# Four tokens to a partition, half-array scores with one Exp over two banks, first batch transposed by the PE, and every engine ordered by a time model

## Chip, cores and metric

The kernel runs on one core of a Trainium2 chip. The metric is the device time of one execution in microseconds (us); medians of several executions are quoted. The engines are PE (TensorE: matmuls, and PEld for its weight loads), ACT (ScalarE), DVE (VectorE), POOL (GpSimd) and SP (SyncE, which here only issues DMAs). Each takes its instructions in a fixed order.

## The reference, cut

```python
# q, k, v: (8 batches, 12 heads, 448 tokens, 64) f32;  w_in: (768, 2048), w_out: (2048, 768) f32
q_n, k_n = rmsnorm(q, g_q), rmsnorm(k, g_k)          # over the 64 of a head
attn = softmax(q_n @ k_n.T / 8)                      # 448 x 448 for each head
x = (attn @ v) as (8*448, 768)
h = x @ w_in
out = (h * clip(h + 3, 0, 6) / 6) @ w_out            # (3584, 768) f32
```

Heads are worked on in 48 pairs, six to a batch. Attention of a batch must be complete before the first h matmul of that batch, because h contracts over all twelve heads.

## The kernel before

448 tokens are cut as 3 x 128 + 64. The 64 left over take a path of their own (loads, norms, a transpose and zero-padded copies for two batches at a time). A pair has seven score matmuls of 128 rows; since a head has 64, the keys are multiplied by a mask, so that the other head's 64 rows are zero.

```python
def pad_pair(P):                       # keys of a pair, twice, each with the other head zeroed
    ...
    nc.vector.tensor_copy(out=kq[:, 2 * SM:], in_=st["rT", b // 2][:, 1, j, e:e + 64])
    for a in range(2):
        nc.vector.tensor_scalar_mul(kp[:, a, :], kq[:, 0:SM], gmask[:, a:a + 1])

def score(P, u):                       # u = 0..6
    ...
    ps = ps_S.tile([128, S], FP32, name="s_ps")
    nc.tensor.matmul(out=ps[:], lhsT=lhsT, rhs=st["qT", P], start=True, stop=True)
    nc.scalar.activation(out=st["e", P][:, u, :], in_=ps[:], func=EXP, bias=zero_c[:], scale=1.0)

def trans_pair(P):                     # every transpose is a DMA transpose
    nc.sync.dma_start_transpose(out=kq[:, 0:2 * SM]..., in_=qks[:]...)

ps_S = pool("ps_S", 3, space=PSUM); ps_X = pool("ps_X", 1, space=PSUM)
ps_R = pool("ps_R", 1, space=PSUM); ps_M = pool("ps_M", 3, space=PSUM)     # M: h and y

# order: SP and POOL by hand; attention and the h and y groups merged by their shares of columns
with tc.manual_schedule(engines={mybir.EngineType.SP, mybir.EngineType.Pool}):
    for b in range(B):
        att = [...]                                                 # attention of batch b
        mlp = mlp_items(h_items(b - 1), y_items(b - 2) ..., 2)      # h of b-1, y of b-2
        for _, fn in merge(att, mlp):
            fn()
    ...
# the weights are loaded between the pairs: w_in at pairs 0 to 6, w_out at pairs 8 to 11
```

Of the kernel before, what the change touches and what calls it, by code (L numbers as in the profile page):

```python
# [10 lines left out]
A_MULT = mybir.AluOpType.mult  # L11
A_ADD = mybir.AluOpType.add
A_MIN = mybir.AluOpType.min
# [4 lines left out]
PSUM = bass.MemoryType.PSUM  # L18


@with_exitstack
def kernel(
# [11 lines left out]
    nc = tc.nc  # L34
# [3 lines left out]
    NPAIR = H // 2  # L38
    NT = 3
    SM = NT * 128  # L40
    SR = S - SM
    NKT = DM // 128
    NFT = DFF // 128
    NU = 2 * NT + 1
    E1 = D + 1
    E2 = 2 * E1
    HALF = DM // 2
    assert SR == 64 and D == 64 and NKT == NPAIR and B % 2 == 0

    pool = lambda name, bufs, **kw: ctx.enter_context(tc.tile_pool(name=name, bufs=bufs, **kw))  # L50
    const = pool("const", 1)


    gq_t = const.tile([128, 1], FP32, name="gq_t")
    gk_t = const.tile([128, 1], FP32, name="gk_t")
    for a in range(2):
        nc.gpsimd.dma_start(out=gq_t[a * 64:(a + 1) * 64, :], in_=g_q.rearrange("(p o) -> p o", o=1))
        nc.gpsimd.dma_start(out=gk_t[a * 64:(a + 1) * 64, :], in_=g_k.rearrange("(p o) -> p o", o=1))
    mask = const.tile([128, 2], FP32, name="mask")
    nc.gpsimd.memset(mask[:], 0.0)  # L60
    nc.gpsimd.memset(mask[0:64, 0:1], 1.0)
    nc.gpsimd.memset(mask[64:128, 1:2], 1.0)
    gprime = const.tile([128, 1], FP32, name="gprime")
    gmask = const.tile([128, 2], FP32, name="gmask")

    def make_gmask():
        nc.vector.tensor_mul(gprime[:], gq_t[:], gk_t[:])
        nc.vector.tensor_scalar(gmask[:], mask[:], gprime[:], 8.0, A_MULT, A_MULT)

    half_c = const.tile([128, 1], FP32, name="half_c")  # L70
    nc.gpsimd.memset(half_c[:], 0.5)
    zero_c = const.tile([128, 1], FP32, name="zero_c")
    nc.gpsimd.memset(zero_c[:], 0.0)

    eps_c = const.tile([128, 1], FP32, name="eps_c")
    nc.gpsimd.memset(eps_c[:], D * 1e-6)
    nc.scalar.preload_act_table_set("natural_log_exp_and_others")

# [3 lines left out]
    NVA = 4  # L82
    va_ring = []
    for i in range(NVA):
        t = const.tile([128, 2, NT, E1], BF16, name=f"va{i}")
        nc.gpsimd.memset(t[:, :, :, D:E1], 1.0)
        va_ring.append(t)
    NVB = 3
    vbd_ring = []
    for i in range(NVB):  # L90
        t = const.tile([128, NPAIR, E2], BF16, name=f"vbd{i}")
        for a in range(2):
            c = a * E1 + D
            nc.vector.tensor_copy(
                out=t[:, :, c:c + 1],
                in_=mask[:, a:a + 1].unsqueeze(1).to_broadcast([128, NPAIR, 1]),
            )
        vbd_ring.append(t)


    qk_pool = pool("qk_pool", 5)
    v_pool = pool("v_pool", 4)
    sq_pool = pool("sq_pool", 2)
    st_pool = pool("st_pool", 8)
    qks_pool = pool("qks_pool", 4)
    rst_pool = pool("rst_pool", 1)
    vr_pool = pool("vr_pool", 2)
    rT_pool = pool("rT_pool", 2)
    kq_pool = pool("kq_pool", 4)
    kp_pool = pool("kp_pool", 3)  # L110
    kbd_pool = pool("kbd_pool", 3)
    e_pool = pool("e_pool", 3)
    rd_pool = pool("rd_pool", 3)
    xn_pool = pool("xn_pool", 3)
    xr_pool = pool("xr_pool", 2)
    xT_pool = pool("xT_pool", 1)
    g_pool = pool("g_pool", 1)
    t_pool = pool("t_pool", 2)
    y_pool = pool("y_pool", 4)
    ps_S = pool("ps_S", 3, space=PSUM)  # L120
    ps_X = pool("ps_X", 1, space=PSUM)
    ps_R = pool("ps_R", 1, space=PSUM)
    ps_M = pool("ps_M", 3, space=PSUM)

    st = {}


    def rstd_of(ssq, n):
        rs = st_pool.tile([128, n], FP32, name="rs", tag="rs")
        nc.scalar.activation(out=rs[:], in_=ssq, func=LN, bias=eps_c[:])  # L130
        nc.scalar.activation(out=rs[:], in_=rs[:], func=EXP, bias=zero_c[:], scale=-0.5)  # L131
        return rs

    def square(out, x, early):
        if early:
            nc.scalar.square(out=out, in_=x)
        else:
            nc.gpsimd.tensor_tensor(out=out, in0=x, in1=x, op=A_MULT)  # L138

    def load_qk(P):  # L140
        b, j = divmod(P, NPAIR)
        hs = slice(2 * j, 2 * j + 2)
        qk = qk_pool.tile([128, 2, 2, NT * D], FP32, name="qk")
        for i, src in enumerate((k, q)):
            nc.sync.dma_start(  # L145
                out=qk[:, i], in_=src[b, hs, 0:SM, :].rearrange("h (p t) d -> p h (t d)", t=NT))
        st["qk", P] = qk

    def load_v(P):
        b, j = divmod(P, NPAIR)  # L150
        vf = v_pool.tile([128, 2, NT * D], FP32, name="vf")
        nc.sync.dma_start(
            out=vf[:],
            in_=v[b, 2 * j:2 * j + 2, 0:SM, :].rearrange("h (p t) d -> p h (t d)", t=NT))
        st["vf", P] = vf

    def load_pair(P):
        load_qk(P)
        load_v(P)

    def norm_pair(P):
        qk = st["qk", P]
        sq = sq_pool.tile([128, 4 * NT * D], FP32, name="sq", tag="sq")
        square(sq[:], qk[:].rearrange("p a h x -> p (a h x)"), P < 4)
        ssq = st_pool.tile([128, 4 * NT], FP32, name="ssq", tag="ssq")
        nc.vector.tensor_reduce(  # L166
            out=ssq[:], in_=sq[:].rearrange("p (n d) -> p n d", d=D), axis=AX_X, op=A_ADD)
        st["ssq", P] = ssq

    def rstd_pair(P):  # L170
        st["rs", P] = rstd_of(st.pop(("ssq", P))[:], 4 * NT)

    def prep_qk(P):
        qk, rs = st.pop(("qk", P)), st.pop(("rs", P))
        rs4 = rs[:].rearrange("p (a h t) -> p a h t", a=2, h=2)
        qks = qks_pool.tile([128, 2, NT, 2, D], BF16, name="qks")
        for i in range(2):
            nc.gpsimd.tensor_tensor(  # L178
                out=qks[:, i].rearrange("p t h d -> p h t d"),
                in0=qk[:, i].rearrange("p h (t d) -> p h t d", d=D),  # L180
                in1=rs4[:, i].unsqueeze(3).to_broadcast([128, 2, NT, D]),
                op=A_MULT)
        st["qks", P] = qks

    def prep_v(P):
        vf = st.pop(("vf", P))
        va = va_ring[P % NVA]
        nc.gpsimd.tensor_copy(  # L188
            out=va[:, :, :, 0:D], in_=vf[:].rearrange("p h (t d) -> p h t d", d=D))
        st["va", P] = va  # L190

    def prep_pair(P):
        prep_qk(P)
        prep_v(P)


    def load_rest(b, i):
        if i == 0:
            st["qkr", b] = rst_pool.tile([128, 2, H, D], FP32, name="qkr")
        for e in range(2):  # L200
            (nc.scalar if b == 0 and i == 1 else nc.sync).dma_start(
                out=st["qkr", b][e * 64:(e + 1) * 64, i],
                in_=(k, q)[i][b + e, :, SM:S, :].rearrange("h p d -> p h d"))

    def load_vrest(b):
        vr = vr_pool.tile([128, NPAIR, D], FP32, name="vr")
        vv = v[b, :, SM:S, :].rearrange("(j a) p d -> a p j d", a=2)
        for a in range(2):
            (nc.scalar if b == 0 else nc.sync).dma_start(out=vr[a * 64:(a + 1) * 64], in_=vv[a])
        st["vr", b] = vr  # L210

    def prep_vrest(b, a):
        vr = st["vr", b]
        vbd = vbd_ring[b % NVB]
        nc.gpsimd.tensor_scalar(
            vbd[:, :, a * E1:a * E1 + D], vr[:], mask[:, a:a + 1], None, A_MULT)
        st["vbd", b] = vbd

    def norm_rest(b, i):
        sq = sq_pool.tile([128, 4 * NT * D], FP32, name="sqr", tag="sq")  # L220
        square(sq[:], st["qkr", b][:, i].rearrange("p h d -> p (h d)"), b == 0)
        ssq = st_pool.tile([128, H], FP32, name="ssqr", tag="ssq")
        nc.vector.tensor_reduce(
            out=ssq[:], in_=sq[:].rearrange("p (n d) -> p n d", d=D), axis=AX_X, op=A_ADD)
        st["ssqr", b, i] = ssq

    def rstd_rest(b, i):
        st["rsr", b, i] = rstd_of(st.pop(("ssqr", b, i))[:], H)

    def prep_rest(b, i):  # L230
        if i == 0:
            st["qkrs", b] = rst_pool.tile([128, 2, H, D], BF16, name="qkrs")
# [11 lines left out]
    def pad_rest(b):  # L244
        e = b % 2
        kbd = kbd_pool.tile([128, NPAIR, 128], BF16, name="kbd")
        for a in range(2):
            nc.vector.tensor_scalar_mul(  # L248
                kbd[:, :, a * 64:(a + 1) * 64], st["rT", b // 2][:, 0, :, e * 64:(e + 1) * 64],
                gmask[:, a:a + 1])  # L250
        st["kbd", b] = kbd


    def trans_pair(P):
        qks = st.pop(("qks", P))
        kq = kq_pool.tile([128, SM + S], BF16, name="kq")
# [354 lines left out]
```

## Time and profile before

| | before |
|---|---|
| time, median of 3 | 531.95 us |
| span of the profiled run | 532.4 us |
| PE busy | 438.5 us (82%) |
| ACT / DVE / POOL busy | 299 / 286 / 214 us |
| columns in all matmuls | 938,500 = 391 us at 2.4 columns/ns |

Busy time of PE overlaps from matmul to matmul, so columns and the distance from start to start say more than its busy share. (2.4 is a round figure: in these traces matmuls of 384 columns start 162 ns apart and those of 512 columns 216 ns, which is 2.37 columns/ns.)

The page's 40 slices (13.3 us each) show in tenths how busy PE was, the clock it was granted, and the mean busy share of the DMA engines. The first nine have full DMA engines.

```profile
...
PE   0365565769988985999889997889978999999996
...
PEclk9987867888999999799998998999989999999999
DMA  9899999996658375435769365446664132120012
```

The windows view gives for each stretch its length, then busy us (and instructions) of PE, PEld, DVE, ACT and POOL, then the PE clock, the DMA share (1 is all 16 engines) and GB/s. The first h matmul of batch 1 starts at 132.8 us, and the last value matmul at 470.0 us.

```profile
...
20.00:60.00 40.00, 24.25 (x193) 13.65 (x192) 30.33 (x42) 25.76 (x54) 28.71 (x33) 0.83 1.08 213
60.00:132.00 72.00, 49.66 (x386) 29.10 (x387) 47.92 (x76) 44.34 (x94) 42.64 (x46) 0.81 0.99 175
132.00:470.00 338.00, 306.23 (x2443) 179.52 (x2442) 178.72 (x377) 209.05 (x403) 132.12 (x142) 0.97 0.53 116
470.00:533.00 63.00, 57.84 (x330) 31.59 (x326) 20.93 (x35) 11.58 (x17) 0.00 (x0) 1.00 0.16 50
...
```

The groups view of the page (line, engine, operation, shapes, count, then busy us, mean ns, idle us before) shows the Exps and the scores of the main path:

```profile
...
L286 ACT ACTIVATE eT<-s_ps,zero_c 128x448 bf16<-128x448 f32 x336 | 202.7, 634 | 79.7 <-PE s_ps L285 78.8
...
L285 PE MATMUL s_ps<-kq,kp 128*128 128x448 bf16 x288 | 109.1, 387 | 30.6 <-DVE kp L269 30.0
...
```

In the timeline of PE (start us, us, instruction) a score matmul of 448 columns (L285) is followed by the next work 0.18 to 0.19 us later, about what 448 columns take at 2.4 columns/ns (187 ns). The four y matmuls ahead of it hold PE for 0.65 us (164.17 to 164.82), four times 162 ns:

```profile
...
163.99 0.35 PE L285 MATMUL s_ps<-kq,kbd 128*128 128x448 bf16 x1
164.17 0.81 PE L388 MATMUL y_ps<-w_out_sb,gT 128*128 128x384 bf16 x4
164.82 0.35 PE L285 MATMUL s_ps<-kq,kp 128*128 128x448 bf16 x1
165.01 0.81 PE L388 MATMUL y_ps<-w_out_sb,gT 128*128 128x384 bf16 x4
...
```

The chain of waits (the work that ended last, followed back) has 45% on PE, 18% on DMA and 12% in which an engine waited for nothing that the profile shows:

```profile
...
PE 45%; DMA 18%; issue 12%; DVE 11%; POOL 8%; SPq 3%; ACT 1%; POOLq 0%
...
```

The groups by shape give the price of ACT work: 128 columns more cost 106 ns.

```profile
...
L374 ACT ACTIVATE t_sb<-h_ps,half_c 128x512 f32<-128x512 f32 x64 | 43.8, 685 | 32.5 <-PE h_ps L369 29.0 <-DVE gT L376 3.4
...
L374 ACT ACTIVATE t_sb<-h_ps,half_c 128x384 f32<-128x384 f32 x64 | 37.1, 579 | 24.6 <-DVE gT L376 16.5 <-PE h_ps L369 7.9
...
```

### The profile page before, as it was taken

To read this page: it belongs to the slowest core of one execution; us is meant where nothing else is said; L and a number is where in the kernel's file an instruction comes from. 1 tells how busy PE (TensorE), PEld (TensorE's weight loads), DVE (VectorE), ACT (ScalarE), POOL (GpSimd) and SP (SyncE) were. 2 spreads that over 40 slices of the span, in tenths; PEclk is the share of its full clock that TensorE was granted. 3 is DMA by queue.
4 is the path that set the end of the run, shared out by engine and by line. 5 is a ranking of instruction groups with operands and counts; after the bars stand their busy time and mean duration, and the time that the engine had idled before them with its cause. 6 is when DMAs were issued, how large, how long until landed. Compare 5 with 4: busy or idle time off the path is not lost.

```text
span 532.4 us, 9016 instructions
## 1 busy us (share of the span) xinstructions
PE 438.5 (82%) x3344; PEld 254.0 (48%) x3344; DVE 285.9 (54%) x545; ACT 298.8 (56%) x583; POOL 214.0 (40%) x247
## 2 busy tenths in 40 slices
PE   0365565769988985999889997889978999999996
PEld 0143332436444553556444554555534566665553
DVE  2686476785645736555545636465545544334421
ACT  3665735757567754566566765576646766623310
POOL 3867676573534655154334643525234410000000
PEclk9987867888999999799998998999989999999999
DMA  9899999996658375435769365446664132120012
GB/s 207 214 224 191 196 140 216 187 186 142 147 140 165 85 185 112 96 96 144 142 139 145 90 170 127 98 98 154 161 109 83 45 90 60 31 76 30 15 64 70
DMA packets 139755, 67.44 MB, mean 127 GB/s; under 512 B 90560, under 2 KB 139712, under 8 KB 139712
## 3 DMA queue, kind: packets, MB, share of 16 engines
q1 hardware_dynamic: 131904, 59.99, 51.2%
q0 software_dynamic: 5440, 6.29, 8.0%
q10 hardware_dynamic: 2368, 0.59, 0.6%
q8 instruction: 26, 0.43, 0.3%
q14 instruction: 17, 0.14, 0.1%
HBM read 45.61 MB, written 11.01 MB: 106 GB/s over the span
## 4 chain that ended last, share of the span: by engine, by line
PE 45%; DMA 18%; issue 12%; DVE 11%; POOL 8%; SPq 3%; ACT 1%; POOLq 0%
PE y_ps L388 20%; PE h_ps L369 14%; DMA kq<-qks 10%; PE s_ps L285 6%; DVE kp L269 4%; PE x_ps L294 3%; POOL sq L138 3%; DMA qkr<-in_q_dram 3%; POOL qks L178 3%; DMA rT<-qkrs 2%; DMA qk<-in_q_dram 2%; DVE xn L313 1%; SPq L145 1%; DVE kq L266 1%; DVE kbd L248 1%
## 5 line engine op out<-in xcount | busy, mean ns | idle before, releaser
L286 ACT ACTIVATE eT<-s_ps,zero_c 128x448 bf16<-128x448 f32 x336 | 202.7, 634 | 79.7 <-PE s_ps L285 78.8
L369 PE MATMUL h_ps<-xT,w_in_sb 128*128 128x384 bf16 (+1 forms) x768 | 190.4, 364 | 20.3 <-DVE gT L376 12.9
L388 PE MATMUL y_ps<-w_out_sb,gT 128*128 128x384 bf16 x896 | 177.7, 331 | 12.9 <-DVE gT L376 12.6
L285 PE MATMUL s_ps<-kq,kp 128*128 128x448 bf16 x288 | 109.1, 387 | 30.6 <-DVE kp L269 30.0
L388 PEld LDWEIGHTS <-gT 128*128 128x128 bf16 x896 | 86.0, 99 | 68.9 <-issue 17.6
L374 ACT ACTIVATE t_sb<-h_ps,half_c 128x384 f32<-128x384 f32 (+1 forms) x128 | 80.9, 632 | 57.0 <-PE h_ps L369 36.9
L369 PEld LDWEIGHTS <-w_in_sb 128*128 128x128 bf16 x768 | 73.7, 100 | 73.2 <-issue 21.9
L188 POOL CAST va<-vf 128x384 bf16<-128x384 f32 x48 | 24.5, 509 | 194.3 <-PE r_ps L297 96.1
L376 DVE SCALAR_TENSOR_TENSOR gT<-t_sb,h_ps 128x384 bf16<-128x384 f32 (+1 forms) x128 | 78.6, 615 | 42.3 <-ACT t_sb L374 41.8
L294 PEld LDWEIGHTS <-eT 128*128 128x128 bf16 x1152 | 68.4, 105 | 65.5 <-issue 31.0
L269 DVE TENSOR_SCALAR kp<-kq,gmask 128x384 bf16<-128x384 bf16 x96 | 57.2, 626 | 78.0 <-DMA kq<-qks 77.9
L178 POOL TENSOR_TENSOR qks<-qk,rs 128x384 bf16<-128x384 f32 x96 | 77.8, 831 | 19.1 <-ACT rs L131 11.9
L294 PE MATMUL x_ps<-va,eT 128*128 128x65 bf16 x864 | 59.4, 203 | 24.8 <-DVE xn L313 20.2
L138 POOL TENSOR_TENSOR sq<-qk 128x768 f32<-128x768 f32 x44 | 64.6, 1468 | 5.8 <-DMA qk<-in_q_dram 5.7
L166 DVE TENSOR_REDUCE ssq<-sq 128x12 f32<-128x768 f32 x48 | 45.4, 946 | 32.5 <-POOL sq L138 24.8
L285 PEld LDWEIGHTS <-kp 128*128 128x128 bf16 x288 | 29.6, 104 | 59.5 <-DVE kp L269 35.2
L394 DVE COPY y_sb<-y_ps 128x384 f32<-128x384 f32 x56 | 31.0, 553 | 45.8 <-PE y_ps L388 45.7
L130 ACT ACTIVATE rs<-ssq,eps_c 128x12 f32<-128x12 f32 x48 | 14.6, 304 | 54.9 <-DVE ssq L166 54.9
L297 PE MATMUL x_ps<-vbd,eT 128*128 128x130 bf16 x144 | 33.6, 233 | 0.4
L313 DVE TENSOR_TENSOR xn<-x_ps,rd 128x384 bf16<-128x384 f32 x48 | 26.6, 554 | 1.2
L266 DVE COPY kq<-rT 128x64 bf16<-128x64 bf16 x48 | 23.3, 486 | 1.3 <-DMA rT<-qkrs 1.2
L294 PE MATMUL r_ps<-va,eT 128*128 128x65 bf16 x288 | 22.3, 201 | 0.1
(37 smaller groups left out, 175.4 us busy)
## 6 DMA issues: line engine op xcount, KB each, us to landing
qk<-in_k_dram SPq DMA_DIRECT2D x48, 192.0 KB, 2.9
qk<-in_q_dram SPq DMA_DIRECT2D x48, 192.0 KB, 2.9
vf<-in_v_dram SPq DMA_DIRECT2D x48, 192.0 KB, 3.6
out_dram<-y_sb SPq DMA_DIRECT2D x48, 192.0 KB, 2.1
w_in_sb<-in_moe_w_in_dram POOLq DMA_DIRECT2D x4, 768.0 KB, 9.8
w_out_sb<-in_moe_w_out_dram POOLq DMA_DIRECT2D x8, 384.0 KB, 6.2
qkr<-in_k_dram SPq DMA_DIRECT2D x8, 192.0 KB, 4.6
out_dram<-y_sb SPq DMA_DIRECT2D x16, 96.0 KB, 2.2
```

The costliest lines, as they stand in the source:

```text
L138: nc.gpsimd.tensor_tensor(out=out, in0=x, in1=x, op=A_MULT)
L166: nc.vector.tensor_reduce(out=ssq[:], in_=sq[:].rearrange("p (n d) -> p n d", d=D), axis=AX_X, op=A_ADD)
L178: nc.gpsimd.tensor_tensor(out=qks[:, i].rearrange("p t h d -> p h t d"), in0=qk[:, i].rearrange("p h (t d) -> p h t d", d=D), in1=rs4[:, i ...
L269: nc.vector.tensor_scalar_mul(kp[:, a, :], kq[:, 0:SM], gmask[:, a:a + 1])
L285: nc.tensor.matmul(out=ps[:], lhsT=lhsT, rhs=st["qT", P], start=True, stop=True)
L286: nc.scalar.activation(out=st["e", P][:, u, :], in_=ps[:], func=EXP, bias=zero_c[:], scale=1.0)
L294: nc.tensor.matmul(out=dst[:, a * E1:(a + 1) * E1], lhsT=eT[:, u, c0:c0 + 128], rhs=va[:, a, t, :], start=(first and a == 0 and t == 0), s ...
L297: nc.tensor.matmul(out=dst, lhsT=eT[:, 2 * NT, c0:c0 + 128], rhs=vbd[:, j, :], start=False, stop=True, skip_group_check=True)
L369: nc.tensor.matmul(out=h_ps[:, 0:n], lhsT=w_in_sb[:, kt, f * 128:(f + 1) * 128], rhs=st["xT", G][:, kt, :], start=(kt == 0), stop=(kt == N ...
L374: nc.scalar.activation(out=t_sb[:, 0:n], in_=h_ps[:, 0:n], func=RELU, bias=half_c[:], scale=1.0 / 6.0)
L376: nc.vector.scalar_tensor_tensor(out=st["gT", G][:, f, :], in0=t_sb[:, 0:n], scalar=1.0, in1=h_ps[:, 0:n], op0=A_MIN, op1=A_MULT)
L388: nc.tensor.matmul(out=y_ps, lhsT=gT[:, f, i * 128:(i + 1) * 128], rhs=w_out_sb[:, f, nh * HALF:(nh + 1) * HALF], start=(f == 0), stop=(f ...
```

## The change

The intent: 448 = 4 x 112, so each partition holds four tokens, 112 partitions are used, and the remainder path disappears (the queries still leave 64 rows of 448 in the values, which are collected over three pairs as before). A score tile has 112 keys. The two heads of a pair lie on the two halves of the partitions and use the two halves of the PE array, into two PSUM banks, and one Exp takes both banks. PSUM is divided anew: two score buffers of two banks, one X, one R, and two banks for M (three before). For pairs 0 to 6 q and k, and for batch 0 the attention output, are transposed by PE; the rest stays with the DMA. All work is first written down as steps with an engine, an assumed duration, a due time and dependences; a list scheduler in the kernel then decides the order on every engine.

```diff
+class Plan:                     # list scheduling: the engine that can start first takes
+    LAT = {...}                 # the ready step with the earliest due time
+    DMA_LATENCY = 1.7           # one DMA, first come first served, xfer us per transfer
+    def order(self): ...
-    NT = 3 ... ps_S 3 banks, ps_M 3 banks
+    T = 4; PT = S // T          # 4 tokens to a partition, 112 partitions
+    S_r = Ring(tiles("S", 2, [128, 2, 512], FP32, psum))
+    M_r = Ring(tiles("M", 2, [128, 512], FP32, psum))
+    NPE = 7                     # pairs whose q and k PE transposes
...
-    nc.tensor.matmul(out=ps[:], lhsT=lhsT, rhs=st["qT", P], start=True, stop=True)
-    nc.scalar.activation(out=st["e", P][:, u, :], in_=ps[:], func=EXP, bias=zero_c[:], scale=1.0)
+    for a in range(2):
+        rows = slice(a * 64, a * 64 + 64)
+        nc.tensor.matmul(out=ps[:, a, 0:S], lhsT=kp[rows, t * PT:t * PT + 128],
+                         rhs=kq[rows, 1, :], start=True, stop=True)
+    ... nc.scalar.activation(out=e[0:PT, t], in_=ps[0:PT, :, 0:S], func=EXP)
...
+    if P < NPE: ... nc.tensor.transpose(out=pt[:, i, ...], in_=qks[0:PT, i, t]..., identity=ident[...])
+    else:       ... nc.sync.dma_start_transpose(out=kq[:]..., in_=qks[0:PT]...)
...
+    for c in range(4):
+        W_in[c] = add("POOL", 0.9, 12 + 6 * c, lambda c=c: load_w_in(c), xfer=5.3)
+    for c in range(8):
+        W_out[c] = add("POOL", 0.9, 36 + 3.5 * c, lambda c=c: load_w_out(c), xfer=2.7)
...
+    with tc.manual_schedule():
+        for s in plan.order():
+            s.fn()
```

Before any run, the built programs show these orders: the scheduler puts all four w_in loads and one w_out load at the head of POOL's queue, and in PE's queue stand 78 h matmuls of batch 0; then pairs 7 to 13 follow, with only two y groups between them, before the first h of batch 1.

## The prediction

> **What bounds it now.** The windows show two stages. From 20 to 120 us the DMA engines are full (share 1.04 to 1.12), PE is busy 64% or less, and its clock is 0.74 from 40 to 100 us; the twelfth of 48 head pairs is normalised at 123.5 us. After 450 us PE has no gap: four 384-column y matmuls take 0.65 us, 0.42 ns a column. The groups hold 938,500 columns (scores 150,500; values 99,800; h and y 344,100 each): 396 us at that rate, inside 532. From 120 to 450 us PE runs at 85% of it; it waits for DVE gT (25 us) and xn (9), and the chain of waits runs through the transposes kq<-qks (10%) and POOL's norm work.
>
> **What changes.**
> 1. Scores: seven zero-padded 448-column matmuls per pair become eight of 64 rows, two on the two halves of the array. If those run together, 86,000 columns replace 150,500: -27 us. The Trainium skill, "TensorEngine Tiling (Array Packing)", Theoretical Speedup, allows up to 2x; its Key Properties say that changing the mode drains the array. No run here shows either. I take back a third for that (192 score pairs at some 50 ns, an estimate): net -18 us. PE transposes add 8,600 columns, 4 us.
> 2. Exp: 336 of 634 ns become 192 of about 0.95 us (0.83 ns a column, from the 384 and 512 column Relus): 203 to 180 us on ACT, not critical later.
> 3. The 64-token remainder path goes: loads in 256 B packets, rT transposes, kq copies (23 us of DVE), kbd (10), half of kp (57), vbd on POOL (20). DVE falls from 286 to about 240 us. Off the critical path later; early it shortens the chain.
> 4. DMA: loads go from 768 B to 1024 B packets, and seven kq and six xT transposes leave the DMA. Its total falls from about 318 to 275 us, most of it early, where it binds.
> 5. M has two PSUM banks, not three: h waits more often for Relu and gT (about 1.9 us). I expect 10 to 25 us of PE waits for gT.
>
> **Sum.** Up to pair 14 DMA must move both weights (42 us by the packets' times), 14 pairs of q, k, v (2.1 us each) and some transposes (12 us): about 84 us. The new PE order has only 46 us of columns before the first h of batch 1, so this stage stays DMA bound and ends near 86 us. Left are 327 us at the measured rate, plus about 10 of mode switches, 18 of waits, 4 each of low clock and drain: about **445 us**, 16% less. Some 35 us come from the early stage, 15 to 20 from the scores, the rest from a denser PE.
>
> Range 424 to 474. Faster by over 2%: 0.97; within 2%: 0.02; slower: 0.01.
>
> **What would show it.** Score pairs starting within a few ns of each other and costing 0.2 to 0.3 us of PE. Exp near 0.95 us, x192. First y work near 55 to 65 us, dense PE from about 86 us at a clock near 1. DMA share near 1 until about 85 us. PE waits for gT of 10 to 25 us. The last 57 us almost unchanged.
>
> **What would make it wrong.** Halves that run one after the other: 36 us more (480). A static order that fits the chip badly, PE blocked behind late w_out chunks or transposes: 20 to 40 us. If two M banks suffice and mode switches are free, 425 is in reach.

## The result, and the profile after

The changed kernel took 482.75 us (median of 4, 481.08 to 483.39); the kernel before took 531.21 us in the runs beside it. The ratio is 0.910, interval 0.904 to 0.917. It is faster, as forecast, but 38 us slower than predicted and outside the range of 424 to 474.

| | before | predicted | after |
|---|---|---|---|
| time, us | 531.95 | 445 | 482.75 |
| first h matmul of batch 1 | 132.8 | 86 | 110.5 |
| from there to the last value matmul | 337.2 | | 306.1 |
| last stretch of h and y alone | 57.5 | "almost unchanged" | 59.5 |
| DMA engine time until the first h of batch 1 | 133 | 84 | 106 |

The times of the rows come from the starts of matmuls in the trace. The spans differ by 51.6 us: 22.3 in the first row of stages, 31.1 in the middle, and 2 lost at the end.

The slices after (12 us each): PE is full, and its clock granted, from the eleventh slice (120 us) on. The DMA engines are full in the second to the fifth, not in the sixth and seventh, and full again from the eighth to the tenth.

```profile
...
PE   0667698968999999999999999999999999999996
...
PEclk9985699998999999999999999999999999999999
DMA  7999984999787845766458567562413312211122
```

The windows after (columns as above). From 110 to 417 us PE is busy 303.5 of 307 us, at clock 1.00 (before: 306 of 338 us at 0.97). From 60 to 110 us the DMA share is 0.72 to 0.87; from 80 to 110 us POOL is busy 27.7 of 30 us:

```profile
...
20.00:60.00 40.00, 28.30 (x283) 17.45 (x282) 18.64 (x37) 20.18 (x32) 23.02 (x26) 0.71 1.15 245
60.00:80.00 20.00, 18.71 (x139) 10.66 (x138) 12.59 (x23) 10.83 (x24) 10.99 (x11) 0.98 0.72 159
80.00:110.00 30.00, 23.61 (x286) 13.28 (x285) 19.31 (x34) 24.81 (x39) 27.72 (x24) 0.98 0.87 179
110.00:417.00 307.00, 303.50 (x2615) 163.81 (x2613) 166.43 (x294) 180.44 (x298) 143.49 (x129) 1.00 0.55 128
417.00:481.00 64.00, 58.25 (x319) 30.86 (x317) 20.11 (x33) 9.56 (x16) 0.00 (x0) 1.00 0.19 51
...
```

The groups that answer to those above: Exp became 192 instructions of 915 ns (I predicted about 950); the score matmuls now number 384, with 64 rows (64*128):

```profile
...
L340 ACT ACTIVATE e<-S 112x896 bf16<-112x896 f32 x192 | 171.4, 915 | 100.6 <-PE S L336 99.3
...
L336 PE MATMUL S<-kq,kp 64*128 64x448 bf16 x384 | 71.2, 384 | 11.1 <-ACT e L340 6.4
...
```

The timeline of PE shows what half-array scores cost. Eight value matmuls (L351) take 0.26 us where h follows (201.62 to 201.88) and 0.35 us where scores follow (199.99 to 200.34). One pair of scores (L336 x2) holds PE for 0.30 us (200.34 to 200.64), two pairs in a row for 0.49 us (204.36 to 204.85):

```profile
...
199.99 0.42 PE L351 MATMUL X<-va,e 112*128 112x65 bf16 x8
200.34 0.36 PE L336 MATMUL S<-kq,kp 64*128 64x448 bf16 x2
200.64 1.15 PE L447 MATMUL M<-xT,w_in_sb 128*128 128x384 bf16 x6
201.62 0.42 PE L351 MATMUL X<-va,e 112*128 112x65 bf16 x8
201.88 0.65 PE L447 MATMUL M<-xT,w_in_sb 128*128 128x384 bf16 x3
...
204.36 0.55 PE L336 MATMUL S<-kq,kp 64*128 64x448 bf16 x4
204.85 2.77 PE L472 MATMUL M<-w_out_sb,gT 128*128 128x384 bf16 x16
...
```

So the two halves do run together: taken over all such starts from 130 to 423 us, the second half starts 3 ns after the first (median), and a further pair 0.20 us later, where one full-array matmul of 448 columns takes 0.19. But the last matmul ahead of a score burst holds PE 95 ns longer than its columns need (258 ns for 384 columns, 162 elsewhere), and the first work behind a burst comes 292 ns after the last score, where a full-array score gives way after 189.

The chain after has 71% on PE, the share of the DMA fell from 18% to 6%, and POOL stands in it with 10%:

```profile
...
PE 71%; POOL 10%; issue 8%; DMA 6%; DVE 2%; ACT 2%; POOLq 0%; ACTq 0%
...
```

Relu lost 89 ns an instruction in either shape. The bias is now a number in the instruction and not a column of a tile. The Trainium skill, "ScalarE: Activation LUTs", What ACT_TABLE_LOAD costs, says that each pointer operand of [128,1] adds about 93 ns; this agrees (579 to 490 and 685 to 596 ns). The Exps lost their bias column too.

```profile
...
L453 ACT ACTIVATE t<-M 128x512 f32<-128x512 f32 x64 | 38.1, 596 | 52.4 <-PE M L447 49.3 <-DVE gT L455 2.2 <-ACT e L340 0.3
...
L453 ACT ACTIVATE t<-M 128x384 f32<-128x384 f32 x64 | 31.4, 490 | 29.4 <-PE M L447 29.4
...
```

### Where the gain came from

For the dense stretch (first h of batch 1 to last value matmul) I counted each matmul's columns at 2.4 per ns and summed what start-to-start distances exceed them by. A score half counts half its columns. A burst is a run of scores with no other matmul between them. Gaps are distances over 250 ns beyond the columns. These are sums over the traces, in us (after the change they miss 0.4 of the 306.1 us of the stretch):

| | before, 132.8 to 470.0 | after, 110.5 to 416.6 |
|---|---|---|
| columns | 284.3 | 265.6 |
| gaps | 36.2 | 4.5 |
| into and out of score bursts | 3.2 | 25.1 (122 bursts) |
| the rest (value, h and y matmuls) | 13.5 | 10.5 |
| sum | 337.2 | 305.7 |

With the change 32 us of gaps went. I put that down to the new order, but no run has the new tiling under the old order. The half-array scores took away 19 us of columns (a little of it because the stretches are not cut at quite the same work) and brought 22 us at the edges of the bursts.

### The profile page after: what moved, and what is told of

It is laid out like the page before. It is cut to its first block, busy times and chain, and to the rows that moved or that the text cites. A ratio compares the mean times of both kernels' runs of the same rounds, so it can differ in the third digit from the quotient of the medians. Undisturbed runs are those within 1.5% of the kernel's fastest.

```text
span 480.8 us, 9258 instructions
## 1 busy us (share of the span) xinstructions
PE 436.2 (91%) x3658; PEld 237.9 (49%) x3658; DVE 246.6 (51%) x429; ACT 253.3 (53%) x421; POOL 220.9 (46%) x218
## 4 chain that ended last, share of the span: by engine, by line
PE 71%; POOL 10%; issue 8%; DMA 6%; DVE 2%; ACT 2%; POOLq 0%; ACTq 0%
PE M L472 30%; PE M L447 25%; PE S L336 8%; PE X L351 6%; POOL qks L280 4%; DMA w_in_sb<-in_moe_w_in_dram 4%; POOL sq L259 3%; PE R L351 2%; DMA kq<-qks 2%; POOL va L288 1%; DVE gT L455 1%; ACT t L453 1%; ACT e L340 1%; DVE kp L314 1%; POOL sq L251 0%
## 5 line engine op out<-in xcount | busy, mean ns | idle before, releaser
L340 ACT ACTIVATE e<-S 112x896 bf16<-112x896 f32 x192 | 171.4, 915 | 100.6 <-PE S L336 99.3
L447 PE MATMUL M<-xT,w_in_sb 128*128 128x384 bf16 (+1 forms) x768 | 170.5, 354 | 4.4 <-DVE y L480 1.9
L472 PE MATMUL M<-w_out_sb,gT 128*128 128x384 bf16 x896 | 161.6, 326 | 0.7 <-DVE gT L455 0.3
L280 POOL TENSOR_TENSOR qks<-qk,rs 112x512 bf16<-112x512 f32 x94 | 97.6, 1057 | 94.1 <-DMA kq<-qks 60.2
L455 DVE SCALAR_TENSOR_TENSOR gT<-t,M 128x384 bf16<-128x384 f32 (+1 forms) x128 | 79.2, 619 | 82.6 <-ACT t L453 82.3
L453 ACT ACTIVATE t<-M 128x384 f32<-128x384 f32 (+1 forms) x128 | 69.5, 543 | 81.8 <-PE M L447 78.6
L259 POOL TENSOR_TENSOR sq<-qk 112x1024 f32<-112x1024 f32 x41 | 78.5, 1919 | 20.1 <-DMA qk<-in_q_dram 13.8
L351 PEld LDWEIGHTS <-e 112*128 112x128 bf16 x1536 | 71.3, 102 | 31.0 <-issue 10.5
L336 PE MATMUL S<-kq,kp 64*128 64x448 bf16 x384 | 71.2, 384 | 11.1 <-ACT e L340 6.4
L351 PE MATMUL X<-va,e 112*128 112x65 bf16 x1152 | 61.9, 201 | 1.9 <-ACT e L340 1.5
L262 DVE TENSOR_REDUCE ssq<-sq 112x16 f32<-112x1024 f32 x48 | 58.0, 1212 | 10.5 <-POOL sq L259 10.3
L336 PEld LDWEIGHTS <-kp 64*128 64x128 bf16 x384 | 18.2, 94 | 51.7 <-issue 41.9
L314 DVE TENSOR_SCALAR kp<-kq,gp 128x448 bf16<-128x448 bf16 x41 | 24.5, 598 | 13.5 <-PE S L336 9.9
L351 PE MATMUL R<-va,e 112*128 112x65 bf16 x384 | 21.7, 201 | 0.0
L269 ACT ACTIVATE rs<-ssq 112x16 f32<-112x16 f32 x48 | 10.4, 216 | 12.7 <-POOL qks L280 6.7
```

The costliest lines, as they stand in the source:

```text
L259: parts.append(add("POOL", 1.95, at - 12, lambda: nc.gpsimd.tensor_tensor(out=sq[0:PT], in0=qk[0:PT], in1=qk[0:PT], op=MULT), *ld, *war))
L262: red = add("DVE", 1.2, at - 8, lambda: nc.vector.tensor_reduce(out=ssq[0:PT], in_=sq[0:PT].rearrange("p i h (t d) -> p (i h t) d", d=D), ...
L280: nc.vector if e == "DVE" else nc.gpsimd).tensor_tensor(
L336: nc.tensor.matmul(out=ps[:, a, 0:S], lhsT=kp[rows, t * PT:t * PT + 128], rhs=kq[rows, 1, :], start=True, stop=True)
L340: x = add("ACT", 0.85, at + step * t / T + 0.2, lambda t=t, ps=ps: nc.scalar.activation(out=e[0:PT, t], in_=ps[0:PT, :, 0:S], func=EXP), s ...
L351: nc.tensor.matmul(out=dst[:, a * E1:(a + 1) * E1], lhsT=e[0:PT, t, a, c0:c0 + 128], rhs=va[0:PT, a, t, :], start=(first and a == 0 and t ...
```

## The experiments

My theory after the trace was this. A: the later part is bound by PE, where each burst of half-array scores costs 0.2 us. Its rival B was my prediction's 50 ns. For the early part I held two theories against each other: DMA bytes bound it, as I had predicted, or the static order and POOL's queue do. Each experiment starts from the changed kernel.

| run | median us | ratio to before, interval | batch 0, us a pair | first h of batch 1 |
|---|---|---|---|---|
| changed kernel | 482.75 | 0.910 (0.904 to 0.917) | 7.3 | 110.5 |
| full_scores | 489.73 | 0.928 (0.924 to 0.933) | 7.1 | 114.8 |
| score_bursts | 488.58 | 0.925 (0.920 to 0.931) | 7.9 | 120.7 |
| dma_trans | 495.15 | 0.938 (0.934 to 0.942) | 5.9, first score at 46.1 us | 125.0 |
| two_exps | 483.55 | 0.915 (0.911 to 0.920) | 7.3 | 111.2 |
| late_wout | 483.02 | 0.910 (0.902 to 0.917) | 6.6 | 112.4 |
| lead6 | 478.87 | 0.901 (0.894 to 0.907) | 7.2 | 114.7 |
| no_weight_dma (wrong result) | 483.54 | 0.916 (0.910 to 0.921) | 6.4 | 110.6 |
| w_model | 479.12 | 0.909 (0.903 to 0.915) | 6.3 | 104.0 |
| act_sq_lead | 476.64 | 0.903 (0.899 to 0.907) | 7.1 | 119.6 |
| npe12 | 478.64 | 0.907 (0.903 to 0.911) | 7.2 | 108.8 |
| nw_wm (wrong result) | 464.07 | 0.875 (0.868 to 0.882) | 4.5 | 94.7 |
| best1 | 478.83 | 0.905 (0.901 to 0.909) | 6.4 | 124.2 |
| paced | 476.46 | 0.899 (0.889 to 0.908) | 4.4 | 110.6 |
| npe12_wm | 475.12 | 0.895 (0.886 to 0.904) | 6.1 | 102.1 |
| npe12_paced | 470.42 | 0.885 (0.875 to 0.894) | 4.4 | 102.1 |

"Batch 0, us a pair" is the time from the first score to the last value matmul of pair 5, over six. Every run gave a right result but the two marked ones. The first four ran on one chip, as did the next two, the next four, the next two and the last three. The kernel before moved from 528 to 532 us between those calls, so differences under about 3 us between rows of different calls should not be read.

Two cautions. The scheduler runs again for every kernel: full_scores, two_exps and no_weight_dma keep the changed kernel's order on PE (matmul for matmul in the traces), but every run that adds, removes or re-times steps also gets a new order on all engines. And most traces of the experiments lack a few matmul records: in full_scores, score_bursts, two_exps and no_weight_dma 23 of the 384 h matmuls of 512 columns are missing, 20 of them (4.3 us) in the dense stretch; the traces before and after have all 384.

### full_scores: whole-array scores, same order

```diff
-    for a in range(2):
-        rows = slice(a * 64, a * 64 + 64)
-        nc.tensor.matmul(out=ps[:, a, 0:S], lhsT=kp[rows, t * PT:t * PT + 128], rhs=kq[rows, 1, :], ...)
+    for a in range(2):        # kp: [128, 2, S + 16], each copy masked to one head
+        nc.tensor.matmul(out=ps[:, a, 0:S], lhsT=kp[:, a, t * PT:t * PT + 128], rhs=kq[:, 1, :], ...)
```

> One thing undone: the scores use the whole array again (eight 448-column matmuls of 128 rows per pair, K zero-padded in two copies, so one more DVE multiplication per pair); the order on every engine stays that of the changed kernel. Theory A (the trace of the changed kernel: two halves start 3 ns apart and do run together, but each burst of scores costs about 100 ns before it and 100 ns after it; 155 bursts): what the halves save (36 us) is about what the bursts cost (31 us), so this comes out within 7 us of the changed kernel, 480 to 490 us. Rival B (my prediction, net gain of 18 us from the halves): 498 to 504 us.

It took 489.73 us, 7 us more than the changed kernel. The timeline of PE shows a pair of scores at 0.38 us (200.92 to 201.30), twice 0.19, and nothing lost behind it:

```profile
...
200.92 0.54 PE L344 MATMUL S<-kq,kp 128*128 128x448 bf16 x2
201.30 0.65 PE L455 MATMUL M<-xT,w_in_sb 128*128 128x384 bf16 x3
...
```

In its dense stretch (114.8 to 423.6 us) the columns on record are 286.7 us; with the 4.3 us of the missing records they are 291.0, 25 more than in the changed kernel. The edges of score bursts cost 1.6 us (23.5 less), and the stretch is 2.7 us longer. The other 4.3 us come before the first h of batch 1, where the additional DVE multiplication of each pair may have a part; they are not shown to be the array's. Theory A holds: what the halves save in columns is about what their bursts cost. The edges are a price of the half-array scores, since the order on PE is the same and they are gone. Rival B expected at least 498 us.

### score_bursts: two score pairs at a time

```diff
-    for t in range(T): take one score buffer; score(t); Exp(t)
+    for t0 in (0, 2):  take both score buffers; score(t0), score(t0 + 1) in one PE step; Exp, Exp
```

> The scores of two quarter-sets are issued together, so that the bursts of half-array matmuls fall from 155 to 95. Theory A (0.2 us for each burst of scores): PE saves up to 12 us, less what it then waits for two free score buffers; 470 to 479 us. Rival B (a change of mode costs about 0.05 us a burst): at most 3 us, 479 to 484 us, or slower because PE waits for two buffers.

It took 488.58 us, 6 us more: outside theory A's range, and B's text allows it ("or slower because PE waits for two buffers"), so the time alone decides nothing. The trace does. In its dense stretch there are 68 bursts (122 before), and their edges cost 13.0 us (25.1 before), again 0.19 us a burst; this stretch, with the same h, y and value work, takes 301.3 us, 4.8 us less than in the changed kernel. Gaps and the rest rose from 15.0 to 26.0 us by the count, but 4.3 of these 11 us are the missing h records. All of the loss lies before the dense stretch: batch 1's first h came 10 us later (120.7 us). So the price of a burst is confirmed; my step from fewer bursts to a shorter time was wrong. PE's step now needs both score buffers free, two Exps stand together on ACT, and the order is new; which of these made the early stage longer is not shown, nor which wait fills each new gap of the dense stretch (the waits view names 5.8 us there).

### dma_trans: no PE transposes

```diff
-    NPE = 7
+    NPE = 0
-    if b == 0:          # PE transposes of the attention output
+    if False:
```

> The PE transposes of the first batch undone: seven kq and six xT transposes go back to the DMA. If the DMA bounds the first 60 us (share 1.15 from 20 to 60 us), its 14 us more of work and the longer chain cost 8 to 20 us: 490 to 502 us. If the early stage is held up by POOL (blocked behind weight loads) and not by the DMA, the change is small: 479 to 488 us.

It took 495.15 us, 12 us more, within the first range. The loss is at the start: the first score comes at 46.1 us (16.5), since the first three transposes of keys and queries held SP's queue 8 to 10 us each (1.2 us elsewhere) and took up to 22.0 us from issue to landing (median of all 3.4). PE transposes, with the order that the scheduler makes for them, are worth 12 us here. That fits a full DMA at the start, but does not show that its bytes set the pace afterwards.

### two_exps: one Exp per bank

```diff
-    nc.scalar.activation(out=e[0:PT, t], in_=ps[0:PT, :, 0:S], func=EXP)
+    for a in range(2): nc.scalar.activation(out=e[0:PT, t, a], in_=ps[0:PT, a, 0:S], func=EXP)
```

> One Exp over two banks undone: two Exps of 112x448 in its place, same order. ACT is busy about 25 us more (2 x 0.52 us against 0.915 us). If PE bounds the kernel after 120 us and ACT has slack, almost nothing changes: 482 to 488 us, all of it before 120 us. If ACT were near critical: over 495 us.

It took 483.55 us, the same within noise; ACT was busy 182 us with 384 Exps of 545 ns (171 us with 192 of 915 ns). One Exp over two banks saves ACT time that nothing waits for. My estimate of 25 us for the saving was too high; it is 11 us. The other 20 us by which Exp fell from 202.7 to 171.4 came without joining the banks: an Exp of 448 columns took 634 ns before and 545 here, 89 ns less, as with Relu.

### late_wout: POOL no longer blocked by weight loads

In the changed kernel's trace POOL stands 10.6 us at loads of w_out that wait for an earlier load, of w_in, to land (the built program has them wait on its semaphore), with the scalings of q and k (L280) behind them. In this timeline of POOL the brackets give the idle time before and what ended it:

```profile
...
24.93 0.72 POOL L215 DMA_DIRECT2D w_out_sb<-in_moe_w_out_dram  x1 [1.91 <-DMA w_in_sb<-in_moe_w_in_dram]
31.21 0.72 POOL L215 DMA_DIRECT2D w_out_sb<-in_moe_w_out_dram  x1 [5.57 <-DMA w_in_sb<-in_moe_w_in_dram]
31.95 1.06 POOL L280 TENSOR_TENSOR qks<-qk,rs 112x512 bf16<-112x512 f32 x1
...
37.65 0.77 POOL L215 DMA_DIRECT2D w_out_sb<-in_moe_w_out_dram  x1 [3.10 <-DMA w_in_sb<-in_moe_w_in_dram]
...
```

```diff
-    W_out[c] = add("POOL", ..., lambda c=c: load_w_out(c), xfer=2.7)
+    W_out[c] = add("POOL", ..., lambda c=c: load_w_out(c), *([VC[c - 1]] if c >= 4 else []), xfer=2.7)
+    # VC[P]: the step that casts v of pair P on POOL
```

> The last four w_out loads are issued later on POOL, after the value casts of pairs 3 to 6, so that POOL no longer stands (10.6 us by the trace) behind loads that wait for w_in to land while the scalings of pairs 3 to 5 stand behind them. Theory A (early stage held by POOL's queue): batch 0 ends 8 to 15 us earlier, first h of batch 1 before 104 us (110.5), total 468 to 478 us. Rival B (early stage is DMA bound, so the place of the issue does not matter): 479 to 486 us.

483.02 us: no change. Batch 0 did end 5 us earlier (55.3 us for 60.4), but pair 11 ended at 104.5 us as before (104.8), and the first h of batch 1 came at 112.4. The time is in rival B's range, and my theory that the blocked queue sets the early stage fell. What came 5 us early waited for something else.

### lead6: all y of batch 0 ahead of h of batch 1

```diff
-    mlp(b, b - 1 if b else None, ..., 2)
+    mlp(b, b - 1 if b else None, ..., 6 if b == 1 else 2)
```

> All six y groups of batch 0 are put ahead of the h groups of batch 1 (two before). From 82 to 110 us PE had only 14 us of columns. Theory A (PE starves there for want of order, not of work): four more y groups (10 us) fit into idle time, 470 to 477 us. Rival B (that stretch is bound by POOL and DMA and the later stretch has slack): 481 to 486 us.

478.87 us, about 4 us less, outside both ranges: 10 us of y columns went into the stretch before the first h of batch 1, which became 4.2 us longer for it (114.7). Part of that stretch was idle for want of work in the order.

### no_weight_dma: weights off the DMA

```diff
-    nc.gpsimd.dma_start(out=w_in_sb[...], in_=moe_w_in[...])      # and w_out
+    pass
...
+    nc.vector.memset(w_in_sb, w_out_sb, 0.01)                      # at the start; wrong result
```

> Wrong result on purpose: the weights are not loaded, DVE sets both weight tiles to one small constant at the start instead, so 42 us of DMA work (by the packets' times) and the 12 loads in POOL's queue are gone; the order on PE stays the same. Theory A (until about 60 us the changed kernel is bound by the DMA, which the weight loads share): batch 0 ends near 42 to 48 us (60.4), first h of batch 1 near 90 to 98 us (110.5), total 462 to 472 us. Rival B (the static order and the work per pair on POOL and ACT hold the early stage, not the DMA): first h of batch 1 after 104 us, total over 475 us. The memset of some 7 to 13 us at the start of DVE may delay the first pair by up to 5 us.

This decided against my prediction that the DMA alone sets the stage. With 36 us of DMA work gone, and the DMA share from 20 to 60 us down from 1.15 to 0.37, the first h of batch 1 came at 110.6 us (110.5), and the time was 483.54 us. Windows:

```profile
...
20.00:60.00 40.00, 29.18 (x312) 17.05 (x313) 22.59 (x45) 23.96 (x38) 23.19 (x24) 0.79 0.37 108
60.00:110.00 50.00, 43.49 (x410) 24.26 (x409) 31.18 (x54) 34.60 (x61) 37.50 (x34) 0.91 0.73 153
...
```

The start came 4.3 us later (the memsets hold DVE for 10.4 us), and batch 0 ran at 6.4 us a pair (7.3), so its last values came at 59.0 us (60.4). The memsets may so hide up to about 4 us of a gain, but not the 24.5 us by which the stage missed. POOL's scalings waited for the reciprocal roots on ACT, as the waits until 110 us show (us, times, longest):

```profile
...
POOL qks L275 <- ACT rs L265: 34.8, 11, 5.5
...
```

And the timeline shows such a turn. DVE stands 2.0 us at the normalisation of an older pair, which waits for its values; behind it in DVE's order stands the sum of squares of a later pair (L257, 38.98 us), behind that ACT's roots and POOL's scaling, which had waited 5.1 us:

```profile
...
36.95 0.20 DVE L371 RECIPROCAL rd<-X 128x6 f32<-128x6 f32 x1 [2.00 <-PE X L346]
...
38.98 1.22 DVE L257 TENSOR_REDUCE ssq<-sq 112x16 f32<-112x1024 f32 x1
...
40.24 0.21 ACT L264 ACTIVATE rs<-ssq 112x16 f32<-112x16 f32 x1 [0.84 <-DVE ssq L257]
...
40.78 2.04 POOL L275 TENSOR_TENSOR qks<-qk,rs 112x512 bf16<-112x512 f32 x2 [5.13 <-ACT rs L265]
...
```

So the preparation of the next pairs stands in order behind the attention of the present one. That batch 0 runs at the length of that chain is my reading of such turns.

### w_model: another order, no other change

```diff
-    load_w_in(c), xfer=5.3       -    load_w_out(c), xfer=2.7
+    load_w_in(c), xfer=1.5       +    load_w_out(c), xfer=0.8      # only what the model believes
```

> Only the order changes: the time model in the kernel is told that the weight loads take 1.5 and 0.8 us (5.3 and 2.7 before), so it mixes the first h groups with the attention of pairs 7 to 13 (before, 78 h matmuls stood in one block while the attention waited). Nothing else is changed, no work is added or removed. Theory A (the block of h in PE's order costs the attention about 20 us of progress): first h of batch 1 near 92 to 102 us (110.5), total 466 to 476 us. Rival B (the pairs arrive no faster than DMA and POOL allow, the order does not matter): first h of batch 1 within 4 us of 110, total 479 to 488 us; PE may now wait in order for pairs that are late.

479.12 us (474.5 to 481.1): first h of batch 1 at 104.0 us, 6.5 earlier. The stage is between the two theories and the time in B's range. The interval overlaps that of the changed kernel, so alone this settles little.

What the new order removes can be seen in the changed kernel's timeline of PE. Its block of 78 h matmuls starts at 65.83 us, when pair 6 has ended, and the scores of pair 7 begin only at 82.46:

```profile
...
65.83 11.60 PE L447 MATMUL M<-xT,w_in_sb 128*128 128x384 bf16 x60
...
82.46 0.55 PE L336 MATMUL S<-kq,kp 64*128 64x448 bf16 x4 [1.15 <-DVE kp L314]
...
```

So pair 7 ends 23 us after pair 6 (89.0 and 65.8 us), and as much without weights (no_weight_dma, 87.7 and 64.6). In w_model it ends 7.4 us after it (68.8 and 61.4), with the h matmuls between later pairs.

### act_sq_lead and npe12

```diff
+    if P < 16: squares of pairs 7 to 15 on ACT (0.6 us each half) and not on POOL     # with lead6's edit
-    NPE = 7
+    NPE = 12                                                                          # npe12 alone
```

> Squares of pairs 7 to 15 on ACT in place of POOL (POOL 1.9 us less per pair, ACT 1.3 us more), together with six y groups of batch 0 ahead of the h groups of batch 1 (478.9 us alone). Theory A (POOL's 4.6 us per pair, busy 95% from 80 to 100 us, paces pairs 7 to 13): another 4 to 8 us, 470 to 475 us. Rival B (ACT with 4.1 us per pair is as near to its limit, so the work only moves): 476 to 483 us.

476.64 us: rival B's range, and 2 us less than lead6, which is not to be read. Either POOL, busy 27.7 of 30 us, was not the limit there, or ACT took its place, as B says; this run does not separate the two.

> The change taken further: PE transposes for pairs 0 to 11 (seven before). Theory A (the DMA and its 3.6 us transposes pace pairs 7 to 11): first h of batch 1 3 to 8 us earlier, 474 to 480 us. Rival B (POOL and ACT pace them, and PE transposes compete for the two M banks): 481 to 490 us.

478.64 us: 4 us less, in theory A's range, but the first h of batch 1 came only 1.7 us earlier, short of what A expected.

### nw_wm: both limits away

The edits of no_weight_dma and w_model together.

> Wrong result on purpose: the weights are constants set by DVE (no weight loads), and the order is that of the kernel whose time model was told of short weight loads. Each alone left the six pairs of batch 0 at 6.3 us a pair (7.3 in the changed kernel). Theory A (two limits of nearly the same height, the DMA and the static order, hide each other): together 4.3 to 5.2 us a pair, first h of batch 1 near 85 to 94 us, total 455 to 466 us. Rival B (the order alone matters, the DMA never did): as with the order alone, first h of batch 1 within 4 us of 104, total 474 to 484 us.

464.07 us, and 4.5 us a pair. Without weights alone: no change. The order alone: 4 us. Both: 19 us. The two limits are nearly as high as each other, and each hides what the other costs; even with the 4 us that the memsets may hide in both runs without weights, the two alone do not add up to the two together. Theory A holds for the time and the pairs; the first h of batch 1, at 94.7 us, is just past its 94.

```profile
...
20.00:60.00 40.00, 29.48 (x369) 17.86 (x370) 35.10 (x55) 28.85 (x49) 35.07 (x34) 0.94 0.53 138
60.00:95.00 35.00, 33.52 (x316) 18.18 (x315) 23.17 (x41) 26.71 (x48) 23.33 (x22) 0.97 0.70 163
...
```

### best1

The edits of w_model and act_sq_lead together.

> Three helpful edits together: the time model told of short weight loads (479.1 us alone), squares of pairs 7 to 15 on ACT and all y groups of batch 0 ahead of the h groups of batch 1 (476.6 us together). Theory A (they fill different holes of the first 110 us): 466 to 473 us. Rival B (they fill the same hole): 474 to 480 us.

478.83 us: rival B's range, and no better than act_sq_lead alone. With this order PE comes to pair 7 early and stands 11.8 us for keys that wait for one DMA transpose (up to 14.5 us). It seems that an order built on a DMA that is too fast pays there what it won; no run tests that by itself.

### paced, npe12_wm, npe12_paced: priority or bytes?

```diff
-    W_in[c]  = add("POOL", 0.9, ..., load_w_in(c), xfer=5.3)
-    W_out[c] = add("POOL", 0.9, ..., load_w_out(c), xfer=2.7)
+    W_in[c]  = add("POOL", 0.9, ..., load_w_in(c), VC[c], xfer=1.5)      # after the cast of v of pair c
+    W_out[c] = add("POOL", 0.9, ..., load_w_out(c), VC[c], xfer=0.8)
```

This is the edit of paced. npe12_wm is `NPE = 12` with the edit of w_model, and npe12_paced is `NPE = 12` with the edit of paced.

> The order of the kernel told of short weight loads, with the same weight bytes, but each weight load is issued on POOL only after a pair's value cast (pairs 0 to 7), so that the loads of q, k and v of the first pairs have the DMA to themselves. Theory A (what the DMA takes from the early pairs is priority, not bytes): batch 0 at 4.6 to 5.5 us a pair as without weights, first h of batch 1 at 92 to 100 us, total 463 to 472 us. Rival B (the bytes bind, whenever they move): batch 0 may be quicker but h of batch 0 or the first y waits for weights, first h of batch 1 at 101 us or later, total 474 to 482 us.

476.46 us (474.0 to 481.0). All bytes are back, but the weights come after the first pairs' loads: batch 0 runs at 4.4 us a pair, as without weights. So in batch 0 it was priority (w_model, whose order is built on the same belief about the weights, ran at 6.3). Then the bill comes: the DMA share stays at 1.0 to 1.2 until 110 us, and PE stands 21.7 us for the keys of pairs whose transposes crawl. Windows, then waits until 110 us:

```profile
...
20.00:60.00 40.00, 27.63 (x355) 17.05 (x354) 24.63 (x46) 27.13 (x47) 38.14 (x38) 0.93 1.21 211
60.00:110.00 50.00, 33.99 (x312) 17.33 (x313) 26.17 (x43) 27.05 (x48) 24.91 (x25) 0.85 1.01 186
...
```

```profile
...
PE S L337 <- DVE kp L315: 21.7, 3, 12.2
DVE kp L315 <- DMA kq<-qks: 20.5, 3, 12.5
...
```

So over the whole early stage the bytes do bind, once the order asks for them early: rival B holds for the stage (first h at 110.6) and for the time.

> PE transposes for pairs 0 to 11 and the time model told of short weight loads. Theory A (under load a DMA transpose of kq is the slow link of pairs 7 to 11 once the order lets them come early): first h of batch 1 at 96 to 103 us, 468 to 475 us. Rival B (the h block that stands again in the order costs what the transposes save): 476 to 483 us.

475.12 us (471.1 to 477.4); the first h of batch 1 at 102.1, so A's stage and the edge of its time.

> Both: paced weight loads and PE transposes for pairs 0 to 11. Theory A (different holes): 462 to 470 us. Rival B: no better than the better of the two alone, within 2 us.

470.42 us (467.5 to 471.8), 5 us less than the better of the two and just outside A's range; 0.885 of the kernel before. Its interval lies wholly below that of the changed kernel; by the ratios it is 2.8% faster (0.885 / 0.910 = 0.972) and the best correct version here. Batch 0 runs at 4.4 us a pair and PE transposes spare pairs 7 to 11 the loaded DMA; the first h of batch 1 comes at 102.1 us with the DMA share over 1 throughout. The traces don't show where its 5 us over npe12_wm come from: that run has the same 102.1 us with batch 0 at 6.1 us a pair, and the two profiled executions, 471.76 and 471.11 us, are alike.

```profile
...
20.00:60.00 40.00, 35.78 (x439) 22.72 (x439) 29.42 (x58) 32.04 (x56) 39.82 (x40) 1.00 1.20 245
60.00:102.00 42.00, 31.99 (x310) 17.63 (x309) 22.31 (x42) 25.37 (x43) 30.95 (x31) 0.88 1.08 191
...
```

## Why the prediction was wrong

Predicted 445, measured 482.75. The profile of the changed kernel has a span of 480.8 us; against it the sum goes like this.

| term | predicted us | measured us |
|---|---|---|
| until the first h of batch 1 | 86 | 110.5 |
| columns after it | 322 | 321.8 (265.6 + 56.2) |
| floor of each matmul above its columns | 5 | 13.8 (10.5 + 3.3 in the last stretch) |
| into and out of score bursts | 10 | 25.1 |
| waits of PE, low clock | 22 | 4.5 |
| drain after the last matmul starts | 4 | 4.8 |
| sum | 449 (stated as 445) | 480.5 |

**The step that failed** is, as the prediction put it, "so this stage stays DMA bound and ends near 86 us". The stage ended at 110.5 us, 24.5 of the 37.8 us missed, and the reasoning was wrong in kind. Taking all weight bytes off the DMA left the end where it was (no_weight_dma, 110.6 us, of which its memsets may be some 4). The static order lay on top of the DMA's limit, and only both together gave much time back (nw_wm, 94.7 us and 19 us less in all). Two features of that order: in batch 0 the preparation of a pair, over DVE, ACT and POOL, stands behind the attention of older ones (6.4 us a pair without weights), and between pairs 6 and 7 stands the block of 78 h matmuls (65.8 to 82.5 us without a score). How the cost divides between the two is not shown; the pace of batch 0 by itself does not set the stage, since late_wout ended batch 0 5 us earlier and the stage no earlier. I had looked at the order only to count the columns ahead of the first h; I did not ask what stood in front of each pair's preparation and scores.

The DMA term was also too small by itself. By 110.5 us the DMA had worked 105.7 us (I said 84): weights 35.6 (I said 42), q, k and v of 19 pairs at 2.5 us each (I said 14 at 2.1), the rest about 21. The 2.5 is not due to the weights: a 1024 B packet took 60 ns in the mean with them and 61 without them (no_weight_dma); only the median moved, 59 to 46. The best order found, npe12_paced, still needed 102 us with the DMA full.

**Step 1, scores: the mechanism right, the size wrong.** The halves run together (second start 3 ns behind the first). The Trainium skill, "TensorEngine Tiling (Array Packing)", Theoretical Speedup, says up to 2x, and a pair of halves indeed takes 0.20 us, about one matmul's 0.19. Its Key Properties say that a change of mode drains the array. The traces do not show a drain as such, but time at the edges that fits one, and its price: 95 ns in and about 100 ns out, 0.2 us a burst. I had put some 50 ns a score pair, a guess that rested on no run. Over 122 bursts of the dense stretch that is 25.1 us (predicted 10 in all), against 25 us of columns saved (full_scores). The net gain of 18 us that I forecast is at most the 2.7 us by which full_scores' dense stretch is longer, and 7 us in the whole time, of which 4.3 are not shown to be the array's.

**Step 2, Exp: the number right, partly by luck.** 915 ns for about 950, and no gain in time (two_exps, within 1 us). But I had the saving of ACT come from joining two banks; that gives 11 of the 31 us, and the other 20 come with the bias that is no longer a column, which I had not named.

**Step 3, the remainder path: right in size.** DVE fell from 286 to 247 us (I said about 240), off the critical path.

**Step 4, DMA: partly right.** The DMA work fell from 133 us at the first h of batch 1 to 106, and in all from 320 us to 286 (I said from 318 to 275). PE transposes are worth 12 us (dma_trans). It was not the only limit, as above.

**Step 5, two banks for M: wrong.** I expected 10 to 25 us of PE waits for gT and put 18 in the sum. The waits of PE for gT from 110 to 417 us do not appear at all, and all gaps together are 4.5 us. In the kernel before, with three banks, these waits were 22.8 us from 132 to 470 us. I take it that the order by due times puts other work between; no run tests it.

**The signs I named:** first y work at 55 to 65 us (was 82.9), dense PE from 86 us (110), clock near 1 afterwards (1.00, right), DMA share near 1 until 85 us (0.72 from 60 to 80, wrong), the last stretch almost unchanged (59.5 for 57.5, near). In "what would make it wrong" I had named an order that fits badly, at 20 to 40 us; it is what happened, with a DMA limit behind it. (One reading of the old profile was off: from 80 to 100 us PE was busy 71%, not 64% or less. Nothing rests on it.) The 480 us that I gave for halves in series is met by chance: they are not in series.

Not settled: what made the early stage of score_bursts longer, how the two features of the order share the cost, and how much of the 102 us of npe12_paced a better order could still take away. The clock is a rival that no run tests: from 40 to 60 us the changed kernel's PE was granted 0.59 of full speed (npe12_paced 1.00, nw_wm 0.88), and whether the slow pairs of batch 0 are in part its effect stays open.

## What to carry to other kernels

Removing a limit by experiment and seeing no change does not show that it was none: two limits of the same height hide each other, so take both away before you conclude. When one part of the array is used for a short burst, count the changes of mode and not only the columns. When an order is static, read what stands in front of each link of the next item's chain on every engine; the time model's picture of the DMA is part of that order (w_model changed nothing else). And before you sum up a trace, count its records against the program: 20 missing matmuls had passed for 4 us of saved columns and added gaps.

## What the Trainium skill lacked or had wrong

- "TensorEngine Tiling (Array Packing)", Key Properties, says that a change of mode drains the array, but gives no price. Here: the matmul ahead takes 95 ns longer, and the work behind comes about 100 ns later (292 for 189 ns), so 0.2 us a burst. For one pair of 448-column matmuls this eats the whole gain of running two at once (0.19 us), though inside a burst the 2x of Theoretical Speedup holds.
- "DMA: Bandwidth & Descriptors", Issuing engines are not separate DMA queues, says that DMAs of different issuers interleave on the same engines. It gives no number for what that costs a transfer. Here the packets hardly show it: until the first h of batch 1 a 1024 B packet issued from SP took 60 ns in the mean (median 59) with weight loads from POOL, and 61 ns (median 46) without them.
- No page gives the loss that a loaded DMA puts on a DMA transpose: here 3.4 us from issue to landing in the median of a run, and up to 22.0 us while the weights were moving (dma_trans).
